# Transposing the row tiles of the later feed-forward blocks on VectorE in 32x32 blocks

## The chip, the cores and the metric

The kernel runs on one core of a Trainium2 chip. The core has five engines that work side by side, each through its own queue in order: TensorE (PE; its weight loads are shown apart as PEld), VectorE (DVE), ScalarE (ACT), GpSimd (POOL), and SyncE (SP), which here only issues DMAs. Engines wait for each other through semaphores. TensorE writes to PSUM, a memory of eight banks; VectorE and ScalarE read PSUM and SBUF. The metric is the device time of one execution in microseconds (us); lower is better.

## The reference, cut to what matters

All arrays are float32. The sequence has L = 2048 rows of D = 512, the feed-forward part has F = 1792 hidden columns.

```python
mod = (_silu(c) @ w_mod).reshape(c.shape[0], 6, 1, -1)
sa, ca, ga, sb, cb, gb = (mod[:, 0], ..., mod[:, 5])
h = _layernorm(x) * (1 + ca) + sa
x = x + ga * _A_ref(h, ...)        # a state-space convolution along the rows, by FFT
h = _layernorm(x) * (1 + cb) + sb
x = x + gb * _B_ref(h, w1, b1, w2, b2)

def _B_ref(x, w1, b1, w2, b2):
    h = jnp.einsum("bsd,df->bsf", x, w1) + b1
    r = jnp.where(h > 0, h, 0)
    h = r * r
    return jnp.einsum("bsf,fd->bsd", h, w2) + b2
```

The change concerns the second half alone: the layer norm before `_B_ref` and how its result gets to TensorE.

## The kernel before, in words

**The work up to the feed-forward part.** Roughly the first half of the span makes the convolution: tables and phases on GpSimd, ScalarE and VectorE, Fourier stages on TensorE. The last of them, `inverse(n)` for n = 0 to 3, gives the 16 row tiles `x2[:, s]` (128 rows x 512 columns each, in the tile `big`), to which the residual is added.

**The feed-forward part** works on four blocks k of 512 rows, that is four row tiles s = 4k to 4k+3 each, and walks the 1792 hidden columns in NF = 14 groups t of 128. A step i = 14k + t consists of `ffn1(i)`, twelve matmuls 128x512 into one PSUM bank, and `ffn2(i-2)`, twelve matmuls 128x512 that add the hidden columns of two steps earlier into four accumulators (`accs`, the tiles tg). Float32 numbers are handled as a sum of two rounded parts, so that each product takes three matmuls: L1047, L1048 and L1050 in `ffn1`, L1067 to L1069 in `ffn2`.

Between the two lie ScalarE and VectorE. For each step ScalarE makes the ReLU out of PSUM (L1053, into `rr`, one of two buffers in the tile xy) and its square, rounded (L1054, the high part); VectorE squares again (L1055) and subtracts the high part (L1056, the low part, in one of three buffers in the tiles w1lc and rw). `ffn2` of that step needs both parts. At the end of a block VectorE takes the four accumulators out of PSUM (L1073, times the gate), adds the residual (L1076), and SyncE stores them. `ffn2` of the next block's first step cannot write an accumulator before it was taken out.

**Making a row tile ready** is `prepare(s)`, the function that is changed. `statistics(s)` (L963 to L966: BN_STATS, BN_AGGR, square root on ScalarE, RECIPROCAL) comes before it. For s of 4 and above, VectorE normalizes the tile into `xn` (L977); GpSimd adds the bias of the output to `x2` (L980); TensorE turns the tile by four transposes 128x128 into one PSUM bank (L984); ScalarE scales and shifts the four pieces into `h32` (L991), and copies the rounded part into the block's `hh` (L995); VectorE subtracts it for the low part `hl` (L997). For these tiles `xn` and `h32` are always the same two buffers, `cs_[0]` and `cs_[1]` (both in the tile xy), so a tile's `h32` must have been read by L997 before the next tile's is written. There are two pairs `hh`, `hl`, used in turn by the blocks, so a block's tiles can be written once the block two before has gone through `ffn1`.

Tiles 0 to 3 (block 0) are prepared before the feed-forward part, with their scaling shared by ScalarE and VectorE; tiles 4 to 15 during it.

**What sets the order.** `keep_order` takes all instructions, gives each a cost (for VectorE 70 ns plus 1.04 ns per element of the free dimension), and lists them engine by engine, the one with the longest way to the end first; the order that results is fixed by dependencies. Instructions named in `in_turn` keep the order of the code among themselves: `turn` puts the matmuls of `ffn1` and `ffn2` there, and the matmuls that `prepare` returns, which the loop calls ahead of steps t = 4, 6, 8 and 10 of the block before the one they belong to. On the other engines the list decides. `tail_bank` hands out four PSUM banks in turn, to `ffn1` and to the transposes.

Of the kernel before, what the change touches and what calls it, by code (L numbers as in the profile page):

```python
# [14 lines left out]
AF = mybir.ActivationFunctionType  # L15
ALU = mybir.AluOpType
# [275 lines left out]
def tile_adaln_ssm_ffn(  # L292
# [18 lines left out]
    nc = tc.nc  # L311
# [37 lines left out]
    ident = ctile("ident", [P, 128])  # L349
# [262 lines left out]
    sbc = ctile("sbc", [P, 4])  # L612
    cbc = ctile("cbc", [P, 4])
# [315 lines left out]
    def tail_bank():  # L929
        tails[0] += 1  # L930
        return tb[tails[0] % 4]
# [36 lines left out]
    def prepare(s):  # L968
        hh, hl = hbuf[s // 4 % 2]
        xn, h32 = (cs_[s], cs_[s]) if s < 4 else cs_[0:2]  # L970
        h32 = h32.rearrange("p (q x) -> p q x", q=4)
        if s < 4:
            nc.vector.scalar_tensor_tensor(
                mv[:, s, 1:2], mv[:, s, 0:1], -1.0, rstd2[:, s : s + 1], op0=ALU.mult, op1=ALU.mult)
            nc.scalar.activation(d4(xn), x2[:, s], AF.Identity, scale=rstd2[:, s : s + 1], bias=mv[:, s, 1:2])
        else:
            nc.vector.tensor_scalar(  # L977
                d4(xn), x2[:, s], mv[:, s, 0:1], rstd2[:, s : s + 1], op0=ALU.subtract, op1=ALU.mult)
        if s > 3:
            nc.gpsimd.tensor_add(x2[:, s], x2[:, s], d4(b2g))  # L980
        tp = tail_bank()
        pe = []
        for q in range(4):
            pe.append(nc.tensor.transpose(tp[:, 128 * q : 128 * q + 128], xn[:, 128 * q : 128 * q + 128], ident))  # L984
        for q in range(4):
            if s < 4 and q > 0:
                nc.vector.tensor_scalar(  # L987
                    h32[:, q, :], tp[:, 128 * q : 128 * q + 128], cbc[:, q : q + 1], sbc[:, q : q + 1],
                    op0=ALU.mult, op1=ALU.add)
            else:  # L990
                nc.scalar.activation(  # L991
                    h32[:, q, :], tp[:, 128 * q : 128 * q + 128], AF.Identity,
                    bias=sbc[:, q : q + 1], scale=cbc[:, q : q + 1])
        ho = hh[:, :, 128 * (s % 4) : 128 * (s % 4) + 128]
        nc.scalar.copy(ho, h32)  # L995
        eng = nc.gpsimd if s < 4 else nc.vector
        eng.tensor_sub(hl[:, :, 128 * (s % 4) : 128 * (s % 4) + 128], h32, ho.bitcast(F32))  # L997
        return pe
# [14 lines left out]
    for s in range(4):  # L1013
        statistics(s)
        prepare(s)
# [64 lines left out]
    for i in range(4 * NF + LAG):  # L1080
        k, t = divmod(i, NF)
        if k < 3 and t in (4, 6, 8, 10):
            turn(prepare(4 * k + 4 + (t - 4) // 2))
        if i < 4 * NF:
            ffn1(i)
        if i >= LAG:
            ffn2(i - LAG)
# [52 lines left out]
```

## Time and profile before

| | before |
|---|---|
| runs, median of 3 | 648.82 us (648.27 to 651.79) |
| profiled execution: span from first to last instruction | 644.7 us |
| profiled execution: own time | not listed; the median is 4.1 us above this span |
| TensorE busy | 586.3 us, 91% of the span |
| VectorE busy | 385.8 us, 60% |
| ScalarE busy | 344.5 us, 53% |
| GpSimd busy | 303.3 us, 47% |
| steps of the feed-forward part | from about 327 us to the end |
| mean granted TensorE clock | 0.979 of full speed |

The profile is one execution, recorded by the hardware. A row of a timeline reads: start, duration, engine, line, operation, output<-input, count, and in brackets the idle time before it and what ended it. Rows with "x2" or more merge neighbours, and give the time from the first one's start to the last one's end. A row of the groups has count, busy time, mean duration of one in ns, and the idle time before them. Busy shares of the whole span are means over very different stages, so the feed-forward part is read by itself.

### The profile page before, as it was taken

Reading aid. Unit: us, or ns where it says so; the run is one execution under the profiler, and the core shown is the slowest. Engines: PE = TensorE matmul, PEld = TensorE weight load, DVE = VectorE, ACT = ScalarE, POOL = GpSimd, SP = SyncE. Lnnn points to the kernel's source line nnn. Section 1 sums busy time; section 2 is a strip of 40 time slices with the busy share of each in tenths; the row PEclk is TensorE's granted clock in tenths of the full one; section 3 lists DMA queues with packets and bytes.
Section 4 is the critical chain, followed back from the end, with each engine's and each line's share of the span. In section 5 each row is a group of like instructions: output and inputs, shape, how many; then the busy total and the mean of one; then the engine's idle time right before and its main releaser. Section 6 shows DMA issues by size and latency. Waiting matters only on the chain.

```text
span 644.7 us, 20841 instructions
## 1 busy us (share of the span) xinstructions
PE 586.3 (91%) x9314; PEld 509.3 (79%) x9314; DVE 385.8 (60%) x659; ACT 344.5 (53%) x632; POOL 303.3 (47%) x243
## 2 busy tenths in 40 slices
PE   1377998899999999897899999999999999999995
PEld 1266987789999899887678888888888888888884
DVE  6999878789797888744679432533325333252223
ACT  5945997979987777461765432244322433222220
POOL 5691999999998988139899200011000100000000
PEclk9999999999999999899599999999999999999999
DMA  9941133030303603654342000100001000010001
GB/s 320 385 134 32 39 68 70 3 68 5 69 4 70 182 5 86 180 185 148 102 133 67 1 0 1 65 1 0 1 2 65 2 0 1 0 66 1 0 1 65
DMA packets 21705, 42.30 MB, mean 66 GB/s; under 512 B 3696, under 2 KB 9200, under 8 KB 20336
## 3 DMA queue, kind: packets, MB, share of 16 engines
q1 hardware_dynamic: 21184, 40.84, 21.0%
q8 instruction: 73, 1.20, 0.8%
q10 hardware_dynamic: 432, 0.14, 0.1%
q14 instruction: 16, 0.13, 0.1%
HBM read 28.39 MB, written 4.19 MB: 51 GB/s over the span
## 4 chain that ended last, share of the span: by engine, by line
PE 49%; DVE 1%; issue 0%; DVEq 0%; ACT 0%
PE tg L1069 8%; PE tg L1068 8%; PE tg L1067 8%; PE ps L1047 6%; PE ps L1048 6%; PE ps L1050 6%; PE kg L1047 2%; PE kg L1048 2%; PE kg L1050 2%; PE ps L943 1%; PE ps L984 1%; DVE xy L987 1%; DVE xy L1073 0%; PE kg L984 0%; DVEq L1125 0%
## 5 line engine op out<-in xcount | busy, mean ns | idle before, releaser
L1055 DVE TENSOR_TENSOR xy<-xy 128x512 f32<-128x512 f32 x56 | 42.7, 762 | 155.9 <-ACT rw L1054 103.9
L1053 ACT ACTIVATE xy<-ps,b1c 128x512 f32<-128x512 f32 x42 | 29.0, 690 | 128.6 <-PE ps L1050 128.6
L980 POOL TENSOR_TENSOR big<-big,lo 128x512 f32<-128x512 f32 x12 | 16.2, 1346 | 156.7 <-DVE xy L977 156.7
L649 PE MATMUL ps<-xy,t_sb 128*64 128x64 f32 x2048 | 67.8, 223 | 2.3 <-issue 2.0
L649 PEld LDWEIGHTS ps<-xy,t_sb 128*64 128x64 f32 x2048 | 64.1, 138 | 5.1 <-issue 2.8
L795 PE MATMUL ps<-e_sb,xy 128*64 128x128 f32 x1024 | 61.2, 274 | 1.1 <-issue 1.1
L795 PEld LDWEIGHTS ps<-e_sb,xy 128*64 128x64 f32 x1024 | 56.7, 140 | 2.4 <-issue 1.3
L641 ACT COPY xy<-ps 128x512 f32<-128x512 f32 x64 | 36.6, 588 | 13.2 <-PE ps L639 12.8
L756 POOL TENSOR_TENSOR rtl<-tables 128x1024 f32<-128x1024 f32 x22 | 43.1, 1961 | 0.2
L786 DVE TENSOR_TENSOR xy<-ps,xy 128x512 f32<-128x512 f32 x64 | 40.1, 681 | 2.3 <-PE ps L649 2.2
L801 DVE COPY big<-ps 128x256 f32<-128x256 f32 x64 | 24.0, 417 | 21.2 <-PE ps L795 21.1
L732 POOL TENSOR_TENSOR llph<-lo,big 128x1024 int32<-128x1024 int32 x16 | 34.3, 2143 | 5.0 <-ACT tg L744 5.0
L732 POOL TENSOR_TENSOR rtl<-lo,big 128x1024 int32<-128x1024 int32 x16 | 34.6, 2162 | 1.8 <-ACT tg L744 1.2
L1047 PE MATMUL ps<-h0h,w1h 128*128 128x512 f32 x88 | 34.9, 397 | 0.4 <-ACT big L954 0.4
L639 PE MATMUL ps<-d_sb,ksb 128*64 128x128 f32 x512 | 34.3, 279 | 1.1 <-DVE ksb L841 1.1
L639 PE MATMUL ps<-d_sb,big 128*64 128x128 f32 x512 | 32.3, 274 | 1.7 <-ACT xy L641 1.0
L776 PE MATMUL kg<-rtl 128*32 128x64 f32 x1408 | 26.3, 223 | 6.4 <-issue 4.5
L1047 PE MATMUL ps<-h,w1h 128*128 128x512 f32 x80 | 31.4, 393 | 0.0
L1053 ACT ACTIVATE xy<-kg,b1c 128x512 f32<-128x512 f32 x14 | 9.6, 689 | 39.3 <-PE kg L1050 39.3
L639 PEld LDWEIGHTS ps<-d_sb,ksb 128*64 128x64 f32 x512 | 28.7, 140 | 2.4 <-DVE ksb L841 1.3
L639 PEld LDWEIGHTS ps<-d_sb,big 128*64 128x64 f32 x512 | 27.8, 137 | 3.1 <-ACT xy L641 1.7
L1056 DVE TENSOR_TENSOR rw<-xy,rw 128x512 fp32r<-128x512 f32 x37 | 28.5, 770 | 2.9
(257 smaller groups left out, 1598.2 us busy)
## 6 DMA issues: line engine op xcount, KB each, us to landing
xy<-xt SPq DMA_DIRECT2D x32, 256.0 KB, 4.4
xy<-xy SPq DMA_DIRECT2D x16, 512.0 KB, 6.3
xy<-w_mod SPq DMA_DIRECT2D x6, 1024.0 KB, 8.5
out_dram<-xy SPq DMA_DIRECT2D x16, 256.0 KB, 2.1
xy<-w SPq DMA_DIRECT2D x14, 256.0 KB, 2.9
raw<-w SPq DMA_DIRECT2D x6, 512.0 KB, 5.8
t_sb<-c_t SPq DMA_DIRECT2D x1, 2048.0 KB, 16.8
i2c<-c_i SPq DMA_DIRECT2D x1, 2048.0 KB, 9.2
```

Source lines behind the costliest of these rows:

```text
L639: nc.tensor.matmul(ps[64 * r : 64 * r + 64, 128 * i : 128 * i + 128], src[:, i], d1_sb[:, r], start=True, stop=True)
L649: nc.tensor.matmul(ps[64 * r : 64 * r + 64, 64 * i : 64 * i + 64].rearrange("p (h q t) -> p q h t", h=2, t=2), t2_sb[:, 8 * g + i, r], src ...
L732: nc.gpsimd.tensor_tensor(ph.rearrange("p d r (a b) -> p (d r) a b", a=4), bc(low_phase[:, us].rearrange("p d r b -> p (d r) b"), 2, 4), b ...
L756: nc.gpsimd.tensor_mul(am[:, 0, :, 32:96].rearrange("p d (v x) -> p d v x", v=2), bc(et[:, 256 + 8 * d0 : 384 + 8 * d0].rearrange("p (y a) ...
L795: nc.tensor.matmul(ps[64 * m : 64 * m + 64, 128 * i : 128 * i + 128], pairs(y)[:, g, i // 2, 64 * m : 64 * m + 64, i % 2], e1_sb[:, h], st ...
L1047: pe.append(nc.tensor.matmul(ps, w1h[:, q, fs], hh[:, q, :], start=(q == 0), stop=False))
L1048: pe.append(nc.tensor.matmul(ps, wl[:, q], hh[:, q, :], start=False, stop=False))
L1050: pe.append(nc.tensor.matmul(ps, w1h[:, q, fs], hl[:, q, :], start=False, stop=(q == 3)))
L1055: nc.vector.tensor_mul(rr, rr, rr)
L1067: pe.append(nc.tensor.matmul(acc, r2l[:, ms], hi_, start=(t == 0), stop=False))
L1068: pe.append(nc.tensor.matmul(acc, r2h[:, ms], lo_, start=False, stop=False))
L1069: pe.append(nc.tensor.matmul(acc, r2h[:, ms], hi_, start=False, stop=(t == NF - 1)))
```

## The change

For tiles 4 to 15, `prepare` makes no TensorE transposes and takes no PSUM bank. VectorE turns the tile instead: sixteen instructions, each of 32 partitions x 4 x 32 elements (128 elements per partition), which transpose 32x32 blocks from `xn` directly into `h32`. ScalarE then scales and shifts `h32` in place, from SBUF. The list that `prepare` returns is empty for these tiles. Tiles 0 to 3 are done as before.

```diff
-        tp = tail_bank()
         pe = []
-        for q in range(4):
-            pe.append(nc.tensor.transpose(tp[:, 128 * q : 128 * q + 128], xn[:, 128 * q : 128 * q + 128], ident))
+        if s < 4:
+            tp = tail_bank()
+            for q in range(4):
+                pe.append(nc.tensor.transpose(tp[:, 128 * q : 128 * q + 128], xn[:, 128 * q : 128 * q + 128], ident))
+            tp = tp.rearrange("p (q x) -> p q x", q=4)
+        else:
+            tp, x4 = h32, xn.rearrange("p (q x) -> p q x", q=4)
+            for g in range(4):
+                for m in range(4):
+                    gs, ms = slice(32 * g, 32 * g + 32), slice(32 * m, 32 * m + 32)
+                    nc.vector.transpose(h32[gs, :, ms], x4[ms, :, gs])
         for q in range(4):
             if s < 4 and q > 0:
                 nc.vector.tensor_scalar(
...
             else:
                 nc.scalar.activation(
-                    h32[:, q, :], tp[:, 128 * q : 128 * q + 128], AF.Identity,
-                    bias=sbc[:, q : q + 1], scale=cbc[:, q : q + 1])
+                    h32[:, q, :], tp[:, q], AF.Identity, bias=sbc[:, q : q + 1], scale=cbc[:, q : q + 1])
```

Six lines are added, so the lines behind it have other numbers in the changed kernel: the transposes are L992, the scaling L998 (was L991), the copy L1001 (L995), the subtraction L1003 (L997), ReLU and square L1059 and L1060 (L1053, L1054), the second square and its subtraction L1061 and L1062 (L1055, L1056), the accumulators' way out L1079 and L1082 (L1073, L1076).

Since the tiles' transposes are no longer tied to TensorE's order, `keep_order` lists the preparation anew. Three places show it. In the rows, xy_91 is the buffer with `xn` and `h32`, xy_93 the one with `rr`, h_5295 the second pair `hh`, `hl`, h0h and h0l the first pair.

First, VectorE in block 0, between the low parts of steps 9 (into w1lc) and 10 (into rw). Before:

```order
L1055 TENSOR_TENSOR xy_93<-xy_93 128x512
L1056 TENSOR_TENSOR w1lc<-xy_93,w1lc 128x512
L977 TENSOR_SCALAR xy_91<-big_83,mv_71,rstd_76 128x512
L997 TENSOR_TENSOR h_5295<-xy_91,h_5295 128x4x128
L1055 TENSOR_TENSOR xy_93<-xy_93 128x512
L1056 TENSOR_TENSOR rw<-xy_93,rw 128x512
```

VectorE at the same place in the changed kernel:

```order
L1061 TENSOR_TENSOR xy_93<-xy_93 128x512
L1062 TENSOR_TENSOR w1lc<-xy_93,w1lc 128x512
L992 STREAM_TRANSPOSE xy_91<-xy_91 32x4x32 x10
L966 RECIPROCAL rstd_76<-rstd_76 128x1
L977 TENSOR_SCALAR xy_91<-big_83,mv_71,rstd_76 128x512
L966 RECIPROCAL rstd_76<-rstd_76 128x1
L964 BN_AGGR mv_71<-st_74 128x2
L963 BN_STATS st_75<-big_83 128x6
L964 BN_AGGR mv_71<-st_75 128x2
L963 BN_STATS st_72<-big_83 128x6
L1061 TENSOR_TENSOR xy_93<-xy_93 128x512
L1062 TENSOR_TENSOR rw<-xy_93,rw 128x512
```

Ten of tile 7's sixteen transposes stand here, and the statistics of later tiles, which stood further ahead.

Second, ScalarE in block 0, around the ReLU and square of step 6 (into w1lc). Before:

```order
L991 ACTIVATE xy_91<-ps_150,sbc,cbc 128x128 x4
L995 CAST h_5295<-xy_91 128x4x128
L1053 ACTIVATE xy_93<-ps_151,b1c 128x512
L1054 ACTIVATE w1lc<-xy_93 128x512
L1053 ACTIVATE xy_93<-ps_152,b1c 128x512
L1054 ACTIVATE rw<-xy_93 128x512
```

ScalarE at the same place in the changed kernel:

```order
L998 ACTIVATE xy_91<-xy_91,sbc,cbc 128x128 x4
L1001 CAST h_5295<-xy_91 128x4x128
L1059 ACTIVATE xy_93<-kg_351,b1c 128x512
L1060 ACTIVATE w1lc<-xy_93 128x512
L965 ACTIVATE rstd_76<-mv_71,epsb 128x1
L1059 ACTIVATE xy_93<-ps_150,b1c 128x512
L1060 ACTIVATE rw<-xy_93 128x512
L998 ACTIVATE xy_91<-xy_91,sbc,cbc 128x128 x4
```

The pattern is the same, but it is tile 4 that is scaled at this place and no longer tile 5, and the scaling waits for VectorE instead of TensorE.

Third, VectorE at the end of block 0, where the accumulators are taken out. Before:

```order
L1056 TENSOR_TENSOR rw<-xy_93,rw 128x512
L1055 TENSOR_TENSOR xy_93<-xy_93 128x512
L1073 TENSOR_TENSOR xy_91<-tg_416,lo 128x512 x2
L1073 TENSOR_TENSOR xy_93<-tg_417,lo 128x512 x2
L1056 TENSOR_TENSOR w1lc<-xy_93,w1lc 128x512
```

VectorE at the same place in the changed kernel, behind the low part of step 14:

```order
L1062 TENSOR_TENSOR rw<-xy_93,rw 128x512
L1003 TENSOR_TENSOR h0l<-xy_91,h0h 128x4x128
L992 STREAM_TRANSPOSE xy_91<-xy_91 32x4x32 x12
L1079 TENSOR_TENSOR xy_91<-tg_416,lo 128x512 x2
L1061 TENSOR_TENSOR xy_93<-xy_93 128x512
L1079 TENSOR_TENSOR xy_93<-tg_417,lo 128x512 x2
L1062 TENSOR_TENSOR w1lc<-xy_93,w1lc 128x512
```

Twelve transposes of tile 10 stand ahead of the first accumulator; in the kernel before, block 2 was not begun here.

More of the change, by code (lines that the diff above doesn't have):

```diff
@@ L987, in prepare @@
                 nc.vector.tensor_scalar(
-                    h32[:, q, :], tp[:, 128 * q : 128 * q + 128], cbc[:, q : q + 1], sbc[:, q : q + 1],
-                    op0=ALU.mult, op1=ALU.add)
+                    h32[:, q, :], tp[:, q], cbc[:, q : q + 1], sbc[:, q : q + 1], op0=ALU.mult, op1=ALU.add)
             else:
                 nc.scalar.activation(
-                    h32[:, q, :], tp[:, 128 * q : 128 * q + 128], AF.Identity,
-                    bias=sbc[:, q : q + 1], scale=cbc[:, q : q + 1])
+                    h32[:, q, :], tp[:, q], AF.Identity, bias=sbc[:, q : q + 1], scale=cbc[:, q : q + 1])
         ho = hh[:, :, 128 * (s % 4) : 128 * (s % 4) + 128]
```

## Prediction

> **What bounds the kernel now.** I read the page first, then the feed-forward part alone, since the change lies there.
>
> ```profile
> span 644.7 us, 20841 instructions
> PE 586.3 (91%) x9314; PEld 509.3 (79%) x9314; DVE 385.8 (60%) x659; ACT 344.5 (53%) x632; POOL 303.3 (47%) x243
> 360.00:380.00 20.00, 20.00 (x94) 16.54 (x93) 7.17 (x11) 7.64 (x16) 2.25 (x2) 1.00 0.00 1
> 400.00:420.00 20.00, 20.00 (x90) 16.54 (x89) 9.20 (x15) 4.67 (x8) 0.00 (x0) 1.00 0.14 52
> 420.00:440.00 20.00, 20.00 (x94) 16.53 (x93) 8.01 (x12) 8.85 (x17) 2.62 (x2) 1.00 0.00 1
> ```
>
> The last three rows are stretches of 20 us: stretch, busy PE, PEld, DVE, ACT, POOL, granted clock. In the feed-forward part TensorE is busy for all 20.00 at full clock, while VectorE works 7 to 9 us. So here a microsecond taken from TensorE shortens the kernel by one, as long as nothing else comes late. The chain that ended last shows what the transposes cost on it.
>
> ```profile
> 412.89 0.91 PE ps L1050 x4
> ...
> 418.33 0.91 PE ps L1050 x4
> ...
> 421.73 0.23 PE tg L1069
> 421.96 0.44 PE kg L984 x4
> 422.39 0.23 PE ps L1047
> ...
> 424.25 0.91 PE ps L1050 x4
> ...
> 429.69 0.91 PE ps L1050 x4
> ```
>
> A step takes 418.33 - 412.89 = 5.44 us; the step with a tile's transposes takes 424.25 - 418.33 = 5.92. A tile's four transposes thus cost 0.48.
>
> **What the change removes.** 12 tiles x 0.48 = 5.8 us on TensorE, all of it on the chain. ScalarE's four scalings read SBUF instead of PSUM:
>
> ```profile
> L1053 ACT ACTIVATE xy<-ps,b1c 128x512 f32<-128x512 f32 x42 | 29.0, 690 | 128.6 <-PE ps L1050 128.6
> L1054 ACT ACTIVATE rw<-xy 128x512 fp32r<-128x512 f32 x37 | 23.4, 633 | 1.2
> ```
>
> Its SBUF-fed square takes 633 ns, its PSUM-fed ReLU 690, so I count no change there.
>
> **What it adds** is 12 x 16 = 192 VectorE instructions of 128 elements per partition. No row shows a transpose on VectorE. The nearest:
>
> ```profile
> L502 DVE TENSOR_SCALAR big<-big 128x128 int32<-128x128 int32 x3 | 0.6, 213 | 0.0
> L623 DVE COPY mt<-ps 128x128 f32<-128x128 f32 x2 | 0.6, 288 | 1.0 <-PE ps L550 1.0
> L987 DVE TENSOR_SCALAR xy<-ps,cbc,sbc 128x128 f32<-128x128 f32 x9 | 3.0, 400 | 1.2 <-ACT xy L991 1.2
> L801 DVE COPY big<-ps 128x256 f32<-128x256 f32 x64 | 24.0, 417 | 21.2 <-PE ps L795 21.1
> 189.82 0.76 DVE L801 COPY big<-ps 128x256 f32<-128x256 f32 x2
> 3.45 0.17 DVE L426 TENSOR_SCALAR kf<-ldt 128x4 f32<-128x4 f32 x1 [2.46 <-DMA ldt<-log_dt]
> 3.65 0.17 DVE L427 TENSOR_SCALAR kf<-kf 128x4 f32<-128x4 f32 x1
> ```
>
> One instruction of 128 elements lasts 213 to 400 ns. What counts is the spacing from start to start. Two independent copies over the same partitions overlap: 0.76 - 0.417 = 0.343 between their starts, 0.07 less than one lasts. An instruction that needs the one before starts 0.03 after its end (3.65 against 3.45 + 0.17). So the spacing lies between 0.213 - 0.07 = 0.14 and 0.400 + 0.03 = 0.43. The plain f32 copy, 288, is nearest in work. With overlap it gives 0.22, without 0.32. I take 0.32: neighbouring transposes read from other partitions each time, and no row shows an overlap for such a pair; that is a judgement, at about two to one.
>
> A rule of the Trainium skill bears on just this. The page "VectorE: DVE Perf Modes", section "Two Vector instructions with no wait between them", gives a model in which an instruction whose input or output starts in another group of 32 partitions than the last one's begins only when every earlier Vector instruction is finished. By that rule the overlapped 0.22 drops out and the sum below stands; without it the sum would be the first rival's. No run here shows it yet. The same page ("The three transpose paths") gives 311 ns for a 128x128 bf16 transpose on VectorE; as an estimate from that figure, a spacing of 0.34 would put the sum 3.1 higher.
>
> **Is there room for 16 x 0.32 = 5.1 us per tile?** By the mean, yes: VectorE idles 11 to 13 of 20 us. But the new order puts the tiles of block 1 close together, and VectorE works strictly in order, so the low part of each step and the emptying of the accumulators stand behind transposes. I add up the longest such stretch, from the second square of step 6 to the first accumulator of block 0. The rows that price it:
>
> ```profile
> 356.11 0.69 DVE L1056 TENSOR_TENSOR rw<-xy,rw 128x512 fp32r<-128x512 f32 x1
> 356.79 0.53 DVE L977 TENSOR_SCALAR xy<-big,mv,rstd 128x512 f32<-128x512 f32 x1
> 357.89 1.36 DVE L997 TENSOR_TENSOR h<-xy,h 128x512 fp32r<-128x512 f32 x1 [0.56 <-ACT h L995]
> 359.85 0.69 DVE L1055 TENSOR_TENSOR xy<-xy 128x512 f32<-128x512 f32 x1 [0.60 <-ACT w1lc L1054]
> 365.29 0.69 DVE L1055 TENSOR_TENSOR xy<-xy 128x512 f32<-128x512 f32 x1 [4.02 <-ACT rw L1054]
> 410.39 2.48 DVE L1073 TENSOR_TENSOR xy<-tg,lo 128x512 f32<-128x512 f32 x4
> L963 DVE BATCH_NORM_STATS2 st<-big 128x6 f32<-128x512 f32 x16 | 10.8, 674 | 3.7 <-POOL big L957 3.6
> L964 DVE BATCH_NORM_AGGREGATE mv<-st 128x2 f32<-128x6 f32 x16 | 2.8, 177 | 0.2
> L966 DVE RECIPROCAL rstd<-rstd 128x1 f32<-128x1 f32 x16 | 2.2, 150 | 4.4 <-ACT rstd L965 4.3
> 357.40 1.30 POOL L980 TENSOR_TENSOR big<-big,lo 128x512 f32<-128x512 f32 x1 [1.94 <-DVE xy L977]
> 358.46 0.69 ACT L1053 ACTIVATE xy<-ps,b1c 128x512 f32<-128x512 f32 x1 [0.60 <-PE ps L1050]
> 355.69 1.51 ACT L991 ACTIVATE xy<-ps,sbc,cbc 128x128 f32<-128x128 f32 x4 [0.80 <-PE ps L984]
> 357.23 0.62 ACT L995 CAST h<-xy 128x512 fp32r<-128x512 f32 x1
> ```
>
> Work in it besides the transposes, each with 0.03 between: nine squares with their subtractions (1.44) 13.0; five normalizations (0.58) 2.9; five low parts of tiles (0.72) 3.6; eight statistics (0.70) 5.6; nine aggregates (0.21) 1.9; ten reciprocals (0.18) 1.8; in all 28.8. L997 took 1.36 instead of 0.69 while GpSimd's L980 ran, 0.67 more; in the new order two of the five L980 meet such an instruction, 1.3. With 90 transposes x 0.32 = 28.8 the stretch needs 58.9 us.
>
> Time it has: the accumulator must be free when `ffn2` of step 14 begins. The last matmuls of `ffn1` of step 16 (the row at 412.89) end at 413.80; four tiles' transposes earlier, that is 411.9; minus one emptying (2.48 / 4 = 0.62), 411.3. It begins after the ReLU of step 6, which in the new order stands behind tile 4's scaling. That waits for four transposes behind the low part of step 5: 356.80 - 0.96 (two tiles' transposes gone from TensorE) + 4 x 0.32 = 357.1; scaling and copy 2.13, ReLU and square 1.4: 360.6. So 50.7 us are there for 58.9: TensorE waits 8.2, plus 0.5 because the third accumulator now stands behind a square: **+8.7**. Part of it comes earlier, at the low parts of steps 10 and 11, which then are more than the two steps behind that `ffn2` allows.
>
> The next stretch, steps 15 to 19: four accumulators 2.5, five squares with subtraction 7.2, three normalizations 1.7, two low parts 1.4, four residual adds (as L1055, 0.65) 2.6, three meetings with L980 2.0, 36 transposes 11.5: 28.9, against 5 x 5.44 + 0.62 = 27.8: **+1.1**. The end of block 1, from `ffn1` of step 27 to the accumulator: ReLU and square 1.4, two squares with subtraction 2.9, two low parts 1.4, a normalization 0.6, one meeting 0.7, 28 transposes 9.0: 16.0, against 3 x 5.44 - 0.62 = 15.7, and the third accumulator again 0.5: about **+1.0** with the small waits between ScalarE and VectorE. After it only 20 transposes follow in five steps, which fit; block 3 has none.
>
> **The clock.** The trace shows what gaps do:
>
> ```profile
> 299.40:302.80 3.40, 1.99 (x154) 1.66 (x146) 0.64 (x2) 0.00 (x0) 3.40 (x3) 1.00 0.07 9
> 302.80:306.20 3.40, 1.85 (x124) 1.46 (x104) 3.29 (x7) 0.83 (x2) 2.82 (x4) 0.68 0.53 150
> 306.20:309.60 3.40, 2.75 (x151) 2.05 (x129) 2.67 (x8) 1.60 (x4) 3.40 (x3) 0.50 0.33 85
> ```
>
> After two stretches with 1.99 and 1.85 of 3.40 busy the granted clock is 0.50. The wait at the end of block 0, some 5 us in one piece, should bring that once. At half clock for one such stretch 1.7 us of work are lost; I take 1.2, since VectorE catches up meanwhile.
>
> **Sum:** -5.8 + 8.7 + 1.1 + 1.0 + 1.2 = +6.2 us on the span, 650.9. The page gives no time outside the span; the median of the runs is 4.1 above it, and nothing there changes: 648.82 + 6.2 = **655.0**. Each 0.01 of spacing is worth (90 + 36 + 28) x 0.01 = 1.5 us.
>
> Costed at nothing:
>
> ```profile
> 325.25 0.69 DVE L963 BATCH_NORM_STATS2 st<-big 128x6 f32<-128x512 f32 x1 [2.31 <-POOL big L957]
> 323.97 6.23 POOL L957 TENSOR_TENSOR big<-big,xy 128x512 f32<-128x512 f32 x5
> ```
>
> The eight transposes ahead of the first square of step 0: VectorE sat idle there 2.31 us before a single BN_STATS. GpSimd getting in the way of the transposes: BN_STATS, with one SBUF input as they have, keeps its 0.69 while GpSimd's L957 runs without a gap. SyncE's queue: loads of residual tiles and of w2 change places by one or two, and what waits for them on ScalarE stands at least a step ahead of its use. The earlier preparation of blocks 2 and 3: their high parts wait for `ffn1` of steps 13 and 27, and are written right behind it.
>
> **Rivals.** (1) The transposes overlap, spacing 0.22: the first stretch needs 30.1 + 19.8 = 49.9, inside its 50.7, everything is hidden, and the whole 5.8 is gained: 643.0. For it speaks L801's overlap; against it that each transpose turns to other partitions. This is the other side; it decides where the waits together cost under 5.8, at a spacing of about 0.29. (2) A spacing of 0.26 to 0.30: waits eat 3 to 8 of the 5.8, and the time stays within 0.5%, 646 to 652. For it speaks an instruction shorter than the 288 of a PSUM copy, as L502 is. (3) A transpose is dearer than a copy, up to the 0.43 from L987: 0.11 x 154 = 17 more, 672. Against it: L987's extra is for PSUM and scalar operands, which a transpose has not.
>
> **How the numbers follow.** A measurement of this kernel tells about 0.5%, 3.2 us. Chances: the forecast (spacing 0.31 to 0.37; its own range 651 to 662) 0.47; rival 1 0.25; rival 2 0.15; rival 3 0.13. Slower 0.60, same 0.15, faster 0.25. The range 642.5 to 668 leaves out the dear end of rival 3 and a gain above 1%, less than 2 in 10.
>
> **What would show it.** Right: L992 about 0.3 us each, next starting after its end; VectorE without a gap from 360 us to the accumulators; TensorE waiting for L1062 of steps 10 and 11 and, longest, for L1079 of block 0; no L984 for tiles 4 to 15. Wrong: L992 starting every 0.22 or less, and TensorE gapless; or waits in places other than these.

## The result, and the profile after

| | before | after |
|---|---|---|
| runs, median of 8 each | 650.61 us (648.27 to 652.41) | 654.95 us (653.76 to 659.32) |
| ratio after/before | | 1.0067, 95% interval 1.0038 to 1.0096 |
| profiled execution: own time / span | not listed / 644.7 us | 654.26 / 652.5 us |

The change makes the kernel 4.3 us slower by the medians. The page of the changed kernel, and its row for the new instructions (busy time, mean ns of one, idle time before them):

```profile
span 652.5 us, 20928 instructions
PE 582.0 (89%) x9266; PEld 504.8 (77%) x9266; DVE 445.1 (68%) x851; ACT 344.8 (53%) x632; POOL 303.8 (47%) x243
L992 DVE STREAM_TRANSPOSE xy<-xy 32x128 f32<-32x128 f32 x192 | 58.1, 303 | 3.1
```

TensorE is busy 4.3 us less than before, and yet the span is longer: it waits. The same stretches of 20 us as in the prediction (stretch, busy PE, PEld, DVE, ACT, POOL, granted clock) show where:

```profile
360.00:380.00 20.00, 20.00 (x90) 16.57 (x89) 18.81 (x48) 8.72 (x18) 2.61 (x2) 1.00 0.00 1
380.00:400.00 20.00, 19.61 (x86) 15.54 (x84) 18.59 (x54) 9.09 (x21) 2.62 (x2) 1.00 0.00 0
400.00:420.00 20.00, 16.62 (x72) 13.44 (x72) 19.09 (x52) 11.52 (x24) 2.99 (x2) 1.00 0.00 1
420.00:440.00 20.00, 18.16 (x73) 14.85 (x74) 19.15 (x42) 7.09 (x14) 2.90 (x2) 0.91 0.14 51
```

VectorE, 7 to 9 of 20 us before, is now full, and TensorE has holes. The waits of TensorE's matmuls in the feed-forward part (what waited, for whom; total, times, longest), and the rows where it happened, the idle time in brackets:

```profile
PE tg L1073 <- DVE xy L1079: 4.8, 2, 3.9
PE tg L1073 <- DVE rw L1062: 1.8, 2, 1.4
394.17 0.50 PE L1073 MATMUL tg<-rw 128*128 128x512 f32 x1 [0.34 <-DVE rw L1062]
401.37 0.50 PE L1073 MATMUL tg<-rw 128*128 128x512 f32 x1 [1.43 <-DVE rw L1062]
421.84 0.50 PE L1073 MATMUL tg<-w,rw 128*128 128x512 f32 x1 [3.85 <-DVE xy L1079]
500.87 0.50 PE L1073 MATMUL tg<-w,rw 128*128 128x512 f32 x1 [0.97 <-DVE xy L1079]
```

These are the low parts of steps 10 and 11, and the accumulators at the ends of blocks 0 and 1. VectorE's timeline (start, duration) shows what stood ahead of them:

```profile
363.70 0.69 DVE L1061 TENSOR_TENSOR xy<-xy 128x512 f32<-128x512 f32 x1
...
394.75 5.05 DVE L992 STREAM_TRANSPOSE xy<-xy 32x128 f32<-32x128 f32 x16
399.83 0.69 DVE L1061 TENSOR_TENSOR xy<-xy 128x512 f32<-128x512 f32 x1
400.63 0.69 DVE L1062 TENSOR_TENSOR rw<-xy,rw 128x512 fp32r<-128x512 f32 x1
...
416.71 3.78 DVE L992 STREAM_TRANSPOSE xy<-xy 32x128 f32<-32x128 f32 x12
420.50 1.29 DVE L1079 TENSOR_TENSOR xy<-tg,lo 128x512 f32<-128x512 f32 x2
```

The sixteen transposes of a tile run as one block of 5.05 us, and the low part that TensorE needs at 401.37 is made right behind it. The accumulators stand behind twelve more, and TensorE starts only when the second of them is out, at 421.84, 0.05 us after the end of the pair (420.50 + 1.29). From 363.70 to 420.50 VectorE waits for another engine once, for 0.27 us; what else it is not busy lies in steps of some hundredths between neighbours. Both blocks of transposes shown belong to tiles of block 2 (tiles 8 and 10): of the 90 transposes in this stretch, 46 are of block 1's tiles 5 to 7 and 44 of block 2's tiles 8 to 10.

**What has to be set aside.** The two profiled executions differ ahead of the changed work too. The first `ffn2` matmul of the feed-forward part, before and after:

```profile
335.53 0.39 PE L1067 MATMUL tg<-w,w1lc 128*128 128x512 f32 x1
339.27 0.39 PE L1073 MATMUL tg<-w,w1lc 128*128 128x512 f32 x1
```

Of the 7.8 us between the spans, 3.74 had passed by then. I do not count that part as the change's: in a kernel below which has no transpose on VectorE before 384.9 us (experiment 5) this matmul starts at 339.11, as late as here, and by its median that kernel takes as long as the one before. The profile before was of an execution shorter than the others: wherever a run's own time and span are both listed, they lie 1.7 to 1.9 us apart, so a span of 644.7 stands for about 646.5 us, 4 under the median. So I compare the traces from this matmul to the end of the span: 644.7 - 335.53 = 309.17 before, 652.5 - 339.27 = 313.23 after, **+4.1**, close to the 4.3 of the medians.

### The profile page after: what moved, and what is told of

The parts are those of the page before. It is cut to its first block, busy times and chain, and to the rows that moved or that the text cites. A ratio compares the mean times of both kernels' runs of the same rounds, so it can differ in the third digit from the quotient of the medians.

```text
span 652.5 us, 20928 instructions
## 1 busy us (share of the span) xinstructions
PE 582.0 (89%) x9266; PEld 504.8 (77%) x9266; DVE 445.1 (68%) x851; ACT 344.8 (53%) x632; POOL 303.8 (47%) x243
## 4 chain that ended last, share of the span: by engine, by line
PE 36%; DVE 12%; ACT 2%; issue 1%; DVEq 0%
PE tg L1073 6%; PE tg L1074 6%; PE tg L1075 6%; DVE xy L992 6%; PE ps L1053 5%; PE ps L1054 5%; PE ps L1056 5%; DVE xy L1061 1%; PE kg L1054 1%; PE kg L1053 1%; PE kg L1056 1%; DVE rw L1062 1%; DVE xy L1079 1%; ACT xy L998 1%; PE ps L943 1%
## 5 line engine op out<-in xcount | busy, mean ns | idle before, releaser
L1061 DVE TENSOR_TENSOR xy<-xy 128x512 f32<-128x512 f32 x56 | 45.2, 807 | 121.9 <-ACT rw L1060 75.2
L1059 ACT ACTIVATE xy<-ps,b1c 128x512 f32<-128x512 f32 x42 | 28.9, 687 | 99.7 <-PE ps L1056 99.7
L980 POOL TENSOR_TENSOR big<-big,lo 128x512 f32<-128x512 f32 x12 | 18.5, 1540 | 133.2 <-DVE xy L977 133.2
L992 DVE STREAM_TRANSPOSE xy<-xy 32x128 f32<-32x128 f32 x192 | 58.1, 303 | 3.1
L998 ACT ACTIVATE xy<-xy,sbc,cbc 128x128 f32<-128x128 f32 x48 | 19.9, 483 | 55.6 <-DVE xy L992 55.6
L1053 PE MATMUL ps<-h0h,w1h 128*128 128x512 f32 x88 | 34.9, 396 | 0.4 <-ACT big L954 0.4
L1062 DVE TENSOR_TENSOR rw<-xy,rw 128x512 fp32r<-128x512 f32 x37 | 31.2, 842 | 3.4
L1053 PE MATMUL ps<-h,w1h 128*128 128x512 f32 x80 | 31.1, 389 | 0.0
```

The lines of the kernel that those rows point to most:

```text
L992: nc.vector.transpose(h32[gs, :, ms], x4[ms, :, gs])
L1053: pe.append(nc.tensor.matmul(ps, w1h[:, q, fs], hh[:, q, :], start=(q == 0), stop=False))
L1061: nc.vector.tensor_mul(rr, rr, rr)
```

## The experiments

My theory: the removal gives TensorE the whole 5.8 us, and the loss comes from where the transposes stand on VectorE; the planner, no longer held by TensorE's order and charging 203 ns for what takes 317, packs block 1's tiles, and the first of block 2 behind them, so densely that low parts and accumulators come late. The main rivals: the removal brings less; or VectorE has not the room at any place. "Rest" is the time from the first `ffn2` matmul to the end of the span; the ratio is to the kernel before, run on the same chip. "The walk" in the expectations steps through the four queues in their order with durations from the traces.

| kernel | median us | ratio, 95% interval | rest us | against before |
|---|---|---|---|---|
| before | 650.1 to 650.6 | 1 | 309.2 | |
| after | 654.95 | 1.0067, 1.0038 to 1.0096 | 313.2 | +4.1 |
| 1 no transposes | 645.55 | 0.9919, 0.9892 to 0.9945 | 305.8 | -3.4 |
| 2 same partitions | 643.05 | 0.9887, 0.9861 to 0.9912 | 303.3 | -5.9 |
| 3 true price | 644.50 | 0.9903, 0.9876 to 0.9930 | 303.4 | -5.8 |
| 4 paced as before | 646.45 | 0.9922, 0.9893 to 0.9951 | 303.7 | -5.5 |
| 5 block 1 on TensorE | 650.10 | 1.0002, 0.9977 to 1.0027 | 308.8 | -0.4 |
| 6 twenty, dense | 667.34 | 1.0274, 1.0238 to 1.0310 | 327.7 | +18.5 |
| 7 twenty, spread | 646.29 | 0.9947, 0.9924 to 0.9969 | 304.9 | -4.3 |
| 8 loops exchanged | 654.59 (one run) | | 314.4 | +5.3 |

**1. No transposes at all.**

```diff
-            tp, x4 = h32, xn.rearrange("p (q x) -> p q x", q=4)
-            for g in range(4):
-                for m in range(4):
-                    gs, ms = slice(32 * g, 32 * g + 32), slice(32 * m, 32 * m + 32)
-                    nc.vector.transpose(h32[gs, :, ms], x4[ms, :, gs])
+            tp = xn.rearrange("p (q x) -> p q x", q=4)
```

> Leaves out the transposing of tiles 4 to 15 altogether: ScalarE scales the untransposed tile into h32, so neither TensorE nor VectorE turns anything. It measures what the removal from TensorE is worth by itself. My theory (a tile's four transposes cost TensorE 0.48 us, all on the chain, and the whole loss comes from VectorE's sixteen instructions per tile): 5.8 us under the kernel before, 0.991 of it, TensorE without a wait from the first ffn1 to the last accumulators, no wait for L1079 at the end of block 0 above 0.5 us. Rival (the removal brings less, because the dense order, the squares and the accumulators get in each other's way even without transposes, or the clock falls): within 2 us of the kernel before, with waits at the same steps 10, 11 and 14 as in the changed kernel.

The ratio of 0.9919 is a gain of 5.3 us on 650.14 (3.6 to 7.0 by its interval); the trace shows 3.4. A wait is left that I did not expect (line numbers are four lower here: L1069 is the first `ffn2` product, L1075 the accumulator):

```profile
416.17 1.28 DVE L1075 TENSOR_TENSOR xy<-tg,lo 128x512 f32<-128x512 f32 x2
417.50 0.50 PE L1069 MATMUL tg<-w,rw 128*128 128x512 f32 x1 [1.05 <-DVE xy L1075]
```

So both sides are partly right: the removal shortens TensorE's own work, but the free order costs something even with no transposes in it: the tiles' scalings and low parts crowd before the end of block 0. Read from TensorE's rows, as is done below for the changed kernel, this end costs 1.8 us, and the end of block 1 another 0.6, where an `ffn2` takes 3.29 us instead of 2.72; -5.8 + 2.4 gives the -3.4. This experiment shows the 5.8 only by that sum; the next two show it whole.

**2. Same partitions for input and output.**

```diff
-                    nc.vector.transpose(h32[gs, :, ms], x4[ms, :, gs])
+                    nc.vector.transpose(h32[gs, :, ms], x4[gs, :, ms])
```

> As the changed kernel, in the same order on every engine, with 192 transposes of the same size, but each reads and writes the same 32 partitions; the blocks are turned but not moved to other partitions (that part of the computation is left out), and the group of partitions changes only at every fourth instruction. Theory (a change of partitions between neighbours is what keeps them from overlapping): inside a run of four they start about 0.23 us apart (0.303 less the 0.07 of overlap that L801's copies show), at a change 0.317, mean 0.25; the 16 take 4.0 us instead of 5.05, the waits at the end of block 0 shrink to under 1 us, and the time is 2 to 5 us under the kernel before. Rival (transposes in a row never overlap): 16 still take 5.05 us, the same waits as in the changed kernel, 4 to 6 us above the kernel before.

The block of sixteen that took 5.05 us, at its place in this kernel, and the line's shortest, median and longest duration in ns:

```profile
389.74 3.58 DVE L992 STREAM_TRANSPOSE xy<-xy 32x128 f32<-32x128 f32 x16
L992 DVE STREAM_TRANSPOSE xy<-xy x192: 256/261/310, 323.5 to 502.2; 32x128 f32<-32x128 f32 x192
```

3.58 us, below the 4.0 of the theory: the mean spacing is (3.58 - 0.26) / 15 = 0.22. Within a group of four a transpose starts 0.19 to 0.24 after the one before it, and that is 0.063 to 0.071 before the one ahead has ended. At a change of group it starts 0.27 after it, not the expected 0.317, and 0.013 to 0.014 after its end; in the changed kernel every transpose of a run starts like that. The transposes at a change last 299 to 310 ns, the others with few exceptions 256 to 268, though all of them read and write the same partitions. So the price comes from the change between neighbours, and not from a transpose moving its block to other partitions: the changed kernel's four in sixteen that move nothing last as long as the rest there, 299 to 309. TensorE has no listed wait from the first `ffn2` on, and the rest is 5.9 shorter than before. Number, order and size of the instructions are unchanged, so what an instruction costs here depends on whether its neighbour works on the same group of partitions; and with the same order the cheaper instruction removes the whole loss.

**3. The true price in the planner.**

```diff
-            t = 70 + 1.04 * (free_size(ins.ins[0]) if type(ins).__name__ == "InstBNStats" else n)
+            t = 317 if "Transpose" in type(ins).__name__ else 70 + 1.04 * (free_size(ins.ins[0]) if type(ins).__name__ == "InstBNStats" else n)
```

> The planner is told that a VectorE transpose takes 317 ns, as measured, instead of the 203 ns of its formula; nothing else is changed, only the order can differ. Theory (VectorE has room enough over a block, and the loss comes from an order that packs block 1's tiles too close because the planner thinks them cheap): the order spreads them, a walk through the queues with the measured durations leaves one wait of 0.4 us, so 5.4 us under the kernel before, ratio 0.992. Rival (VectorE has not the room in block 0 whatever the order, since 12 tiles, statistics and squares meet there): the waits for L1062 and L1079 stay and the time is within 3 us of the changed kernel, that is 2 to 6 above the kernel before.

5.6 us faster than before by the medians, and 5.8 by the trace. The stretch in which the changed kernel lost most, and VectorE ahead of the first accumulators of block 0:

```profile
400.00:420.00 20.00, 20.00 (x89) 16.37 (x88) 19.10 (x51) 7.98 (x17) 1.32 (x1) 1.00 0.00 1
410.75 3.14 DVE L992 STREAM_TRANSPOSE xy<-xy 32x128 f32<-32x128 f32 x10
413.92 0.69 DVE L1061 TENSOR_TENSOR xy<-xy 128x512 f32<-128x512 f32 x1
414.53 1.88 DVE L1079 TENSOR_TENSOR xy<-tg,lo 128x512 f32<-128x512 f32 x3
```

VectorE is as full as in the changed kernel (19.10 against 19.09 of 20 us), and TensorE has no hole. The planner now puts fewer transposes ahead of the accumulators and low parts, since it counts them dearer: 90 instead of 108 ahead of the first accumulator, 55 instead of 80 ahead of the low part of step 11. The rival, that VectorE has not the room, falls.

**4. The old pace.** The price stays at 203; the planner gets one more pair per transpose, the last matmul before the place where the code calls `prepare`.

```diff
+    [before[no[b]].add(no[a]) for a, b in PAIRS]; after = [[] for _ in groups]
...
+                    PAIRS.append((PES[-1], nc.vector.transpose(h32[gs, :, ms], x4[ms, :, gs]).ins.name))
...
+        in_turn.update(x.ins.name for x in pe); PES.extend(x.ins.name for x in pe)
```

> The planner keeps its price of 203 ns, but a tile's transposes may be listed only behind the matmuls of the step ahead of which the code calls for them (steps 4, 6, 8, 10 of the block before), as the TensorE transposes were held in the kernel before. Theory (the loss is the lost pacing: without a place in TensorE's order the tiles of block 1 crowd together): spread over the block, one wait of about 1.8 us at ffn2 of step 10, otherwise hidden; 3.9 us under the kernel before, ratio 0.994. Rival (capacity of VectorE): two tiles' worth, 5.07 per two steps of 10.9 us, with 2.9 of squares and the rest is too much at any place, and the time is at or above the kernel before.

3.7 us faster by the medians, 5.1 by the ratio, 5.5 by the trace, with no listed wait in it. The wait of 1.8 us that the walk gave at step 10 did not come; the walk was wrong there. Either the pace or the price is enough to get the gain; both act on the order alone.

**5. Block 1 back on TensorE.**

```diff
-        if s < 4:
+        if s < 8:
             tp = tail_bank()
```

> Only the four tiles of block 1 are turned on TensorE again, in their old places; the tiles of blocks 2 and 3 stay on VectorE, 128 transposes in all, the planner's price unchanged. Theory (the largest term of the sum, the first stretch with its 8.7 us and the clock's 1.2, hangs on block 1's tiles; the later terms do not): TensorE gains 8 x 0.48 = 3.8 us; the waits at the ends of block 0 and block 1 keep about 1 us each with 0.5 for the third accumulator, and nothing is waited for at steps 10 and 11: 0 to 2 us under the kernel before. Rival (the loss is spread over all blocks): two thirds of the changed kernel's loss stay, about 3 us above the kernel before.

No change against the kernel before that this measurement can tell: the interval reaches from 1.5 us under it to 1.8 over it, which takes in the theory's end at 0 and leaves out the rival's 3. The waits of its TensorE, and their two places:

```profile
PE tg L1073 <- DVE xy L1079: 1.9, 2, 1.0
418.33 0.50 PE L1073 MATMUL tg<-w,rw 128*128 128x512 f32 x1 [0.95 <-DVE xy L1079]
496.33 0.50 PE L1073 MATMUL tg<-w,rw 128*128 128x512 f32 x1 [0.97 <-DVE xy L1079]
```

The waits at steps 10 and 11 and the one of 3.85 are gone with block 1's transposes. What is left is about 1 us at the ends of blocks 0 and 1, where blocks 2 and 3 are prepared; with the slower start behind it each of these ends costs 1.7 us, read as below, and -3.8 + 2 x 1.7 gives the -0.4 of the table.

**6 and 7. Twenty transposes per tile, dense and spread.** Four of the sixteen are made twice. In 6 the planner's price per transpose is scaled by 0.8, in 7 it is 317.

```diff
-                for m in range(4):
+                for m in (0, 0, 1, 2, 3):
```

> As the changed kernel, with four of a tile's sixteen transposes made twice (20 per tile, 240 in all, same result), at a planner's price scaled by 0.8, so that a tile has the same price and the order stays nearly as dense. Theory (in the dense order each more microsecond of VectorE in the three stretches is paid in full): 154 x 0.25 x 0.317 = 12.2 us over the changed kernel by the prediction's sum, 14 by the walk through the queues, so 16 to 19 us over the kernel before, ratio about 1.026. Rival (VectorE has idle time around, so part of it is hidden): under 6 us over the changed kernel.

> The same 240 transposes, 20 per tile, with the planner's price of 317 ns each, as in the run with the true price. Theory (the place of the transposes decides, not their sum on VectorE): spread, the 15.2 us of additional VectorE work are nearly hidden; the walk gives one wait of 3.2 us at the beginning of block 1 and 2.6 us under the kernel before, 19 or more below the dense order with the same instructions. Rival (VectorE's capacity): as slow as the dense order, or at least above the kernel before.

The waits of TensorE in the dense kernel, then in the spread one, with VectorE's time around the end of block 0 in each:

```profile
PE tg L1073 <- DVE xy L1079: 10.4, 2, 7.1
PE tg L1073 <- DVE rw L1062: 4.7, 4, 2.7
PE tg L1073 <- DVE w1lc L1062: 1.4, 1, 1.4
420.00:440.00 20.00, 12.93 (x46) 10.12 (x45) 19.28 (x44) 6.96 (x14) 3.36 (x2) 0.74 0.04 13
```

```profile
PE kg L1053 <- ACT h L1001: 1.3, 1, 1.3
420.00:440.00 20.00, 20.00 (x89) 16.54 (x89) 18.93 (x46) 6.14 (x11) 1.68 (x1) 1.00 0.07 27
```

With the same 240 instructions of 303 ns the kernel takes 667.34 us in one order and 646.29 in the other. In the dense order 48 more transposes, 15.2 us of VectorE, lengthen the rest by 14.4, and the kernel is 17.1 us above the one before, inside what the theory gave. Spread, TensorE waits once, for 1.3 us instead of the walk's 3.2, and the kernel stays 3.9 us ahead of the one before. This is the clearest of the runs: what the transposes cost is set by their place.

**8. The loops exchanged**, so that the input keeps its group of partitions for four instructions and the output changes.

```diff
-            for g in range(4):
-                for m in range(4):
+            for m in range(4):
+                for g in range(4):
```

> As the changed kernel with the two loops exchanged: four neighbours read the same 32 partitions and write to another group each time (in the changed kernel four neighbours write the same group and read another each time). Theory (a change of group on the input or on the output keeps the next from overlapping): 16 in a row still take 5.05 us, 0.317 each, and the time is that of the changed kernel. Rival (only the input's group matters): 0.2 apart within four, 16 in 3.6 us, and the waits go as in the run with the same group for both.

```profile
393.83 5.05 DVE L992 STREAM_TRANSPOSE xy<-xy 32x128 f32<-32x128 f32 x16
PE tg L1073 <- DVE xy L1079: 4.8, 2, 3.9
```

A block of sixteen in this kernel and its longest waits: the same 5.05, the same 4.8. A change on either side is enough. The rest is 1.2 us longer than in the changed kernel; 0.8 of it is the `ffn2` behind the long gap, which takes 5.28 us instead of 4.44, at a granted clock of 0.62 and 0.50. The Trainium skill's rule that the prediction weighed ("VectorE: DVE Perf Modes", "Two Vector instructions with no wait between them") says the same: an instruction whose input or output starts in another group of 32 partitions is held until all earlier ones are finished. The traces agree in the three cases they have: 0.317 between starts with the output's group kept and the input's changed, 0.317 the other way round, a mean of 0.22 where both are kept for three neighbours in four; only in the last case does one begin before the one ahead has ended.

## Why the prediction was right, point by point

The direction and the mechanism were right. That the time agrees to 0.1 us is luck: I forecast +6.2 on a median of 648.82, the runs show +4.3 on one of 650.61. The 4.1 us that I took for time outside the span are not that (it is 1.7 to 1.9 in the runs that list both); the sum does not suffer, since it adds a difference to the median. Where that difference is too large, the terms show one by one.

**The removal, -5.8.** Right: with no wait left, the rest is 5.8 and 5.9 us shorter than before (experiments 3 and 2).

**The spacing, 0.32 by judgement.** Right: 5.05 us for sixteen that last 303 ns, so (5.05 - 0.303) / 15 = 0.317. Its two parts were off in opposite directions: an instruction lasts 303 ns, not 288, and the next starts 0.014 after its end, not 0.03. The overlapped 0.22 of the first rival exists, and makes the kernel fast, as experiment 2 shows; it needs neighbours that read and write the same groups, and no two of a tile's sixteen do. The Trainium skill's page "VectorE: DVE Perf Modes" ("The three transpose paths") puts 311 ns on a 128x128 bf16 transpose, of 32x32 blocks only. With the blocks moved as well, and in f32, a piece of 128x128 takes a quarter of the sixteen here, 5.05 / 4 = 1.26 us.

**The first stretch, +8.7, and the clock, +1.2.** Right in place, 1.8 too high together. TensorE's loss can be read from its rows: the last matmul of `ffn1` ahead of each wait, the wait (above), and the first of the next `ffn1`.

```profile
392.76 1.07 PE L1056 MATMUL ps<-h0l,w1h 128*128 128x512 f32 x4
397.06 0.39 PE L1053 MATMUL ps<-h0h,w1h 128*128 128x512 f32 x1
398.88 1.07 PE L1056 MATMUL ps<-h0l,w1h 128*128 128x512 f32 x4
404.23 0.39 PE L1053 MATMUL kg<-h,w1h 128*128 128x512 f32 x1
416.92 1.07 PE L1056 MATMUL ps<-h,w1h 128*128 128x512 f32 x4
426.28 0.40 PE L1053 MATMUL ps<-h,w1h 128*128 128x512 f32 x1
```

Undisturbed, four of L1056 take 0.91 and an `ffn2` half a step, 2.72: 3.63 from the one row to the other. Here it is 4.30, 5.35 and 9.36: lost 0.67 + 1.72 + 5.73 = **8.1**, against 9.9 for stretch and clock. Of this the clock has 1.7 (below) instead of 1.2, and the stretch 6.4 instead of 8.7. The term that was too large is VectorE's work in the stretch, 58.9. From 363.70 to 420.50 it took 56.8, with the 90 transposes that I had counted (28.6 of it). The small instructions are why:

```profile
402.48 0.15 DVE L966 RECIPROCAL rstd<-rstd 128x1 f32<-128x1 f32 x1
402.60 0.18 DVE L964 BATCH_NORM_AGGREGATE mv<-st 128x2 f32<-128x6 f32 x1
402.70 0.66 DVE L963 BATCH_NORM_STATS2 st<-big 128x6 f32<-128x512 f32 x1
403.28 0.15 DVE L966 RECIPROCAL rstd<-rstd 128x1 f32<-128x1 f32 x1
```

I had added 0.18 + 0.21 + 0.70 = 1.09 for such a group. It comes again after 0.80: each begins before the one ahead has ended. Counted from start to start over the stretch, statistics, aggregates and reciprocals take 7.5 us instead of the forecast 9.3, and the five normalizations 2.3 instead of 2.9. The two meetings with GpSimd were there, as counted: L1061 at 371.00 took 1.34 and L1062 at 414.46 took 1.61, 1.6 us more than alone, against 1.3. With these 0.3 and the 0.27 of waiting on the one side, and 0.2 less for the transposes on the other, the missing 2.1 are accounted for. The time that was there, 50.7, came out as forecast, but by two errors: the stretch began 0.6 earlier than I had it (beside the 3.74 set aside above), and TensorE needs two accumulators out, not one, which takes as much away again.

**The clock by itself.** The one long gap brought the slow clock, as forecast:

```profile
416.80:420.20 3.40, 1.19 (x6) 0.65 (x4) 3.25 (x12) 1.32 (x2) 0.00 (x0) 1.00 0.00 0
420.20:423.60 3.40, 1.76 (x5) 1.42 (x6) 3.39 (x7) 0.00 (x0) 0.00 (x0) 0.81 0.00 0
423.60:427.00 3.40, 3.40 (x12) 2.66 (x12) 3.29 (x8) 1.49 (x4) 0.86 (x1) 0.69 0.00 0
```

TensorE is busy for 1.19 and 1.76 us of the first two stretches; in the second the granted clock is 0.81, in the one behind it 0.69. The `ffn2` that runs there takes 426.28 - 421.84 = 4.44 instead of 2.72: 1.7 of the 5.73. That the third accumulator comes behind a square shows no cost beside it.

**Steps 15 to 19, +1.1.** Wrong: no wait appears there. VectorE's work was as I had set it, 28.9: from the first accumulator to the end of the low part of step 19 it takes 447.96 + 1.61 - 420.50 = 29.1.

```profile
447.96 1.61 DVE L1062 TENSOR_TENSOR rw<-xy,rw 128x512 fp32r<-128x512 f32 x1
```

The step that failed is the time, 27.8. The `ffn2` that needs this low part starts at 450.78, so 30.3 were there: 0.7 more because TensorE had waited for two accumulators, and the 1.7 that its slow clock gives VectorE. Without the slow clock about 0.5 of wait would be left; that is reckoned from this trace, no run takes it apart.

**The end of block 1, +1.0.** Right in place, 0.7 too low, by the same reading:

```profile
498.84 1.07 PE L1056 MATMUL kg<-h0l,w1h 128*128 128x512 f32 x4
499.53 1.29 DVE L1079 TENSOR_TENSOR xy<-tg,lo 128x512 f32<-128x512 f32 x2
504.16 0.40 PE L1053 MATMUL ps<-h0h,w1h 128*128 128x512 f32 x1
```

From the one to the other 5.32, 1.69 more than 3.63: the wait of 0.97, 0.15 more at its start, and an `ffn2` of 504.16 - 500.87 = 3.29 instead of 2.72, in which the third accumulator comes late. The missing 0.7 is the second accumulator: I had TensorE start when the first was out, but it starts at 500.87, 0.05 after the end of the pair, and so it does at every such wait of these kernels (experiment 5: 418.27 and 418.33). The first two lie in one tile, tg_416; whether that is the reason, no run shows.

Sum by the trace: -5.8 + 8.1 + 0 + 1.7 = +4.0, against the +4.1 measured. By the forecast: +6.2. The waits together cost 9.8, not 12.0; at the forecast's 1.5 us for each 0.01 of spacing, an estimate, they fall to 5.8 at 0.29, the point that the first rival named.

**What was costed at nothing.** GpSimd does not get in the way of the transposes: eight of them keep their spacing, (2.50 - 0.30) / 7 = 0.314, while GpSimd runs without a gap:

```profile
324.96 2.50 DVE L992 STREAM_TRANSPOSE xy<-xy 32x128 f32<-32x128 f32 x8
320.85 5.14 POOL L1003 TENSOR_TENSOR h0l<-xy,h0h 128x512 fp32r<-128x512 f32 x4
325.95 3.70 POOL L957 TENSOR_TENSOR big<-big,xy 128x512 f32<-128x512 f32 x3
```

ScalarE's four scalings take 1.65 us out of SBUF (359.99 in this trace) where four took 1.51 out of PSUM, so "no change" was off by 0.14 a tile. ScalarE, SyncE's queue and the high parts of blocks 2 and 3 appear in none of the waits of TensorE's matmuls listed above. What I did treat as given was the order itself: the forecast held for this order, and two edits of the planner alone turn the same 192 instructions into a gain.

**The best version** is the true price (experiment 3): 0.9903 of the time before, 0.9876 to 0.9930, for one number in the planner. Experiment 2 is not faster than it beyond the intervals, and it leaves work out.

## What to carry to other kernels

When work moves to an engine whose mean load is low, add up the stretch in which that engine is in order ahead of something the bound engine needs: here an engine that was 60% busy as a mean became 94% busy for the 60 us from 360 on. If a planner sets the order, give it the measured price of the new instruction, and replace any tie that the old instruction had to the pace of the bound engine; otherwise a removal that is right by itself can come out as a loss. Compare the same instructions in two orders before concluding that an engine has no room.

## What the runs showed of the hardware that was not expected

- A VectorE transpose of 32 partitions x 128 f32 elements, in 32x32 blocks, takes 303 ns, and 0.317 us from start to start, where each one reads or writes another group of partitions than the one before. Where both stay it starts some 0.066 before the one ahead has ended and mostly lasts 256 to 268; sixteen with three changes took 3.58 us instead of 5.05.
- Short independent VectorE instructions overlap with their neighbours: a reciprocal, an aggregate and a BN_STATS came every 0.80 us, though 0.15 + 0.18 + 0.66 = 0.99 are needed one after the other.
- A wait costs TensorE more than its own length: the 0.97 at the end of block 1 cost 1.7 with the late third accumulator, the 3.85 at the end of block 0 cost 5.7 with the slow clock behind it.
